# Eight feed-forward tiles narrowed among the experts, the second product two steps behind, five load buffers, remainders on VectorE

## The chip, the cores and the metric

The kernel runs on one NeuronCore of a Trainium2 chip. Its engines work side by side, each through its own instructions in order: TensorE (PE), VectorE (DVE), ScalarE (ACT), GpSimd (POOL) and SyncE (SP, which only issues transfers). The metric is the device time of one execution in microseconds (us), as a median of several runs. The profile is that of one execution.

## The reference

The program chains a linear attention with decay, a mixture of experts with one expert for each token, and a gated feed-forward layer. Only the last two are touched here:

```python
# x: 3072 tokens of width 512; 8 experts, w1 512x1024, w2 1024x512
for e in range(E):
    mask = e_idx == e
    h = np.maximum(x[mask] @ w1[e], 0.0)
    ye = h @ w2[e]
    out[mask] = gate_w[mask, None] * eom[mask, e, None] * ye
# then, with d_ff 1536
rms = np.sqrt(np.mean(x * x, axis=-1, keepdims=True) + 1e-06)
xn = x / rms * rms_g
g = xn @ w_gate
silu = g * (1.0 / (1.0 + np.exp(-g)))
val = xn @ w_val
return (silu * val @ w_out)
```

## The kernel before

All of it is one program whose order on each engine is the order in which the code is written. Products are made of three matmuls on 32-bit operands split into a rounded part (`h`) and a remainder (`l`): high times high, high times remainder, remainder times high. Four stages follow each other: attention with routing (0 to 157 us), the experts (157 to 463 us), the turn to the feed-forward layer, and the feed-forward layer itself on four pairs of blocks of 384 tokens.

**Experts.** The experts are taken in the order of their load, with `CAPS` = 448, 456, 432, 416, 408, 400, 384 and 368 columns for w = 0 to 7. Each has eight steps f. A step t = 8w + f is `up` (12 matmuls into PSUM bank f % 2, then ACT writes `hh` and DVE the remainder `hl`) and then `down` (12 matmuls into banks 4 to 7) of the step before. Behind f = 0 of the next expert `evac` copies banks 4 to 7 into `ys`. `settle` spreads the normalisation of the expert before over the steps: squares on ACT, sums and `halve` on DVE, `mean` (two matmuls with a tile of ones, then a square root on ACT) at f = 4, `inverse` (reciprocals on DVE) and `scale`. `turn` at f = 5 and 6 transposes the next expert's tokens.

**Expert weights.** Each of the 64 steps needs one weight tile of 128 x 1024. SP loads it into one of three buffers `raw`, ACT rounds it into slot `wt`, POOL writes the remainder beside it (`split_weights`). There are 12 slots; six lie outside the attention's memory.

**Feed-forward weights.** There are 36 tiles (j = 0 to 35) of 128 x 512 in 64-bit floating point, which arrive as pairs of integers and are narrowed on the chip: `narrow_steps` gives two ACT operations (L192, L193) and four DVE operations (L195, L201, L204, L207), and behind them come a rounding on ACT (L180) and a remainder on POOL (L181). Two tiles share a slot; tiles 3f, 3f + 1 and 3f + 2 make the weights of step f. Tiles 0 to 6 are narrowed during expert 7, tiles 7 to 13 in the turn, the rest in the first pair of blocks, three in each step f (`uconvs_to(17 + 3 * (f - 3), share)`, where a share says into how many parts the remaining work is still to be cut).

**Turn and feed-forward.** A step of a pair is `gate(b0, f)` (24 matmuls: 12 into bank 0, 12 into bank 1; ACT takes the silu of bank 0 in L825, DVE multiplies with bank 1 in L826, ACT rounds in L827, DVE makes the remainder in L828), `project` of the other block (9 matmuls), `gate(b1, f)` and `project(b0, f)`. So a gate's first half may start when ACT's L825 of the gate before has read bank 0, and its second half when DVE's L826 has read bank 1. In the turn the gates of steps 0 to 2 are interleaved with the last expert's normalisation (L369 is a reciprocal); its scaling is four multiplications on POOL (L964), once both reciprocals are there.

Of the kernel before, what the change touches and what calls it, by code (L numbers as in the profile page):

```python
# [25 lines left out]
KB = DM // 128  # L26
# [14 lines left out]
NPRE = 6  # L41
NSLOT = 12
NRAW = 3
NDIRECT = 4
# [60 lines left out]
def fused_kernel(  # L105
# [60 lines left out]
    def wslot(t):  # L166
        return wt[t % NSLOT if t < NWT + NSLOT else t - NWT]

# [17 lines left out]
    def narrow_steps(v, u, before):  # L186

        v = v.rearrange("p (c t) -> p c t", t=2)
        lo, hi, b = v[:, :, 0], v[:, :, 1], fl_b[0]

        def first():
            ACT.activation(out=u, in_=hi, func=AF.Abs, scale=2.0 ** -20)  # L192
            ACT.activation(out=u, in_=u, func=AF.Abs, bias=mid)  # L193
            before()
# [8 lines left out]
            ),  # L203
            lambda: DVE.scalar_tensor_tensor(  # L204
# [6 lines left out]

    state = {"load": 0, "work": 0, "end": NPRE}
    steps, after = [], []

    def loads_to(t):
        while state["load"] < min(t, state["end"]):
            n = state["load"]
            r = raw[n % NRAW]  # L220
            if n < NWT:
                load_expert_weights(r, window_expert(n // NF), n % NF)
            else:
                SP.dma_start(out=r.bitcast(I32), in_=wm2[n - NWT].bitcast(I32))
            state["load"] += 1

    def flush():
        for do in after:
            do()
        after.clear()  # L230

    def next_tile():
        n = state["work"]
        r = raw[n % NRAW]
        state["work"] += 1
        loads_to(n + NRAW - (n < NWT))
        if n < NWT:
            steps.append(lambda: split_weights(wslot(n), r))
        else:
            j = n - NWT  # L240
            u = fl_u[j % 2]
            narrow = narrow_steps(r.bitcast(I32), u, flush)
            last = lambda: after.append(lambda: split_weights(wslot(NWT + j // 2), u, j % 2))
            steps.extend([*narrow[:3], lambda: (narrow[3](), last())])

    def work_to(t, share=1):

        t = min(t, state["end"])
        left = len(steps) + sum(1 if n < NWT else 4 for n in range(state["work"], t))
        for _ in range(-(-left // share)):  # L250
            if not steps:
                next_tile()
            steps.pop(0)()

    def convs_to(t):
        work_to(min(t, NWT))

    def uconvs_to(n, share=1):
        work_to(NWT + n, share)
        if n >= NU and not steps:  # L260
            flush()


    class Experts:
# [41 lines left out]
        def up(self, w, f, n, wtile):  # L306
# [9 lines left out]
            hh, hl = self.hh[f % 2][:, 0:n], self.hl[f % 2][:, 0:n]  # L316
# [3 lines left out]
        def down(self, f, n, wtile):  # L320
            hh, hl = self.hh[f % 2][:, 0:n], self.hl[f % 2][:, 0:n]
# [120 lines left out]
    with ExitStack() as es:  # L442
# [335 lines left out]
        state["end"] = NWT + NU  # L778
# [33 lines left out]
    def gate(b, f, halves=None):  # L812
# [14 lines left out]
        ACT.activation(out=ah, in_=a, func=AF.Copy)  # L827
        DVE.tensor_tensor(out=al, in0=a, in1=f32(ah), op=ALU.subtract)  # L828
# [36 lines left out]
    hh = [m1.tile([128, CMAX], F32R, name=f"hh{i}") for i in range(2)]  # L865
    hl = [m1.tile([128, CMAX], F32R, name=f"hl{i}") for i in range(2)]
    ys = [m1.tile([128, KB, CMAX], F32, name=f"ys{i}") for i in range(2)]
    sq = [m1.tile([128, CMAX], F32, name=f"sq{i}") for i in range(KB)]
    ex = Experts(hh, hl, ys, sq, sq[1])
    pend = None  # L870

    def settle(w, f, bank):

        n = CAPS[w]
        if f == 0:
            ex.square(0, n)
            ex.square(1, n)
        elif f == 1:
# [267 lines left out]
```

## Time and profile before

| | |
|---|---|
| median of 3 runs (lowest, highest) | 1105.97 us (1104.77, 1106.41) |
| the profiled execution | 1100.29 us |
| its span, first to last instruction | 1098.6 us |
| PE busy | 1049.3 us (96%) |
| DVE busy | 505.8 us (46%) |
| ACT busy | 387.9 us (35%) |
| POOL busy | 336.7 us (31%) |
| mean granted clock of PE | 0.993 of full speed |

A busy PE is not yet a PE at its best pace: its matmuls are pipelined, so the pace is read from the distance of their starts. The idle time before an instruction and what ended it stand in brackets in a timeline. A share of busy time is a mean over stages with different limits, so each stage is read by itself.

### The profile page before, as it was taken

How to read it: one execution, taken by the hardware profiler on the slowest of the kernel's cores; microseconds unless marked ns; L12 is line 12 of the kernel's file. 1: busy time of each engine (PE TensorE's matmuls, PEld its weight loads, DVE VectorE, ACT ScalarE, POOL GpSimd, SP SyncE). 2: the span in 40 equal slices, each digit the busy share in tenths (PEclk: the TensorE clock that was granted, in tenths of full speed). 3: DMA queues.
4: the chain of work that ended last, by engine and by line, in shares of the span. 5: the costliest groups of instructions: out<-in, count | busy, mean ns of one | idle time of the engine just before them, and what ended most of it. 6: DMA issues, size and time to landing. Idle time of an engine off the chain costs nothing.

```text
span 1098.6 us, 16579 instructions
## 1 busy us (share of the span) xinstructions
PE 1049.3 (96%) x6537; PEld 973.3 (89%) x6538; DVE 505.8 (46%) x980; ACT 387.9 (35%) x742; POOL 336.7 (31%) x269
## 2 busy tenths in 40 slices
PE   6899989999999999898899999999999999999995
PEld 5787779989999999897888999999999999999995
DVE  3565652465665667988888631121321212212111
ACT  2443444453443454554555421111311112211111
POOL 2343457856646664624333220000110000200002
PEclk9999989999999999999999999999999999999998
DMA  7899746555645645533434120000200000100001
GB/s 267 231 261 251 191 119 199 151 162 166 201 151 165 205 153 164 148 103 102 135 120 127 64 88 8 1 1 1 87 29 1 1 1 30 58 1 1 1 1 61
DMA packets 47145, 115.43 MB, mean 105 GB/s; under 512 B 12893, under 2 KB 24413, under 8 KB 44242
## 3 DMA queue, kind: packets, MB, share of 16 engines
q1 hardware_dynamic: 39026, 96.01, 29.9%
q0 software_dynamic: 4864, 12.50, 3.2%
q10 hardware_dynamic: 3168, 5.77, 1.5%
q8 instruction: 53, 0.87, 0.3%
q14 instruction: 34, 0.28, 0.1%
HBM read 91.76 MB, written 23.11 MB: 105 GB/s over the span
## 4 chain that ended last, share of the span: by engine, by line
issue 40%; PE 37%; DVE 9%; ACT 4%; DMA 4%; POOL 3%; SPq 1%; POOLq 0%; DVEq 0%
PE ps L311 12%; PE ps L324 11%; DMA qkv<-att 3%; PE ps L818 3%; DVE fb L204 2%; PE ps L553 2%; POOL out_dram L851 2%; PE ps L525 2%; PE ps L519 1%; POOL w L181 1%; DVE fb L201 1%; PE ps L297 1%; PE ps L836 1%; PE ps L495 1%; ACT fu L192 1%
## 5 line engine op out<-in xcount | busy, mean ns | idle before, releaser
L818 PE MATMUL ps<-zh,w 128*128 128x384 f32 x960 | 257.0, 338 | 7.3 <-ACT a L825 7.3
L826 DVE TENSOR_TENSOR a<-a,ps 128x384 f32<-128x384 f32 x96 | 53.0, 552 | 322.5 <-PE ps L818 316.4
L818 PEld LDWEIGHTS ps<-zh,w 128*128 128x128 f32 x960 | 175.4, 189 | 12.9 <-ACT a L825 10.3
L181 POOL TENSOR_TENSOR w<-raw,w 128x1024 fp32r<-128x1024 f32 x64 | 155.7, 2447 | 91.5 <-ACT w L180 90.8
L818 PE MATMUL ps<-zl,w 128*128 128x384 f32 x480 | 161.8, 337 | 0.0
L818 PE MATMUL ps<-xh,w 128*128 128x384 f32 x576 | 154.8, 339 | 4.0 <-DVE a L826 2.6
L311 PE MATMUL ps<-xh,w 128*128 128x448 f32 (+7 forms) x512 | 149.7, 354 | 0.0
L836 PE MATMUL ps<-w,ah 128*128 128x512 f32 x564 | 145.3, 393 | 0.0
L851 POOL DMA_INDIRECT out_dram<-xw,perm x10 | 9.9, 992 | 420.6 <-ACT xw L849 417.6
L827 ACT ACTIVATE ah<-a 128x384 fp32r<-128x384 f32 x94 | 49.3, 525 | 202.9 <-DVE a L826 202.9
L836 PEld LDWEIGHTS ps<-w,ah 128*128 128x128 f32 x564 | 104.7, 188 | 16.3 <-ACT ys L346 0.4
L825 ACT ACTIVATE a<-ps 128x384 f32<-128x384 f32 x96 | 46.7, 487 | 201.4 <-PE ps L818 201.3
L818 PEld LDWEIGHTS ps<-xh,w 128*128 128x128 f32 x576 | 104.9, 188 | 7.3 <-DVE a L826 3.3
L324 PE MATMUL ps<-hh,w 128*128 128x448 f32 (+7 forms) x512 | 106.7, 350 | 0.0
L311 PEld LDWEIGHTS ps<-xh,w 128*128 128x128 f32 x512 | 95.3, 188 | 3.2
L818 PE MATMUL ps<-xl,w 128*128 128x384 f32 x288 | 97.0, 337 | 0.0
L324 PEld LDWEIGHTS ps<-hh,w 128*128 128x128 f32 x512 | 93.8, 188 | 2.9
L818 PEld LDWEIGHTS ps<-zl,w 128*128 128x128 f32 x480 | 90.7, 189 | 2.0
L311 PE MATMUL ps<-xl,w 128*128 128x448 f32 (+7 forms) x256 | 90.0, 351 | 0.0
L181 POOL TENSOR_TENSOR w<-fu,w 128x512 fp32r<-128x512 f32 x36 | 54.3, 1508 | 113.2 <-ACT w L180 113.2
L836 PE MATMUL ps<-w,al 128*128 128x512 f32 x282 | 80.0, 392 | 0.0
L828 DVE TENSOR_TENSOR al<-a,ah 128x384 fp32r<-128x384 f32 x94 | 52.5, 559 | 55.5 <-ACT ah L827 55.5
(151 smaller groups left out, 1441.6 us busy)
## 6 DMA issues: line engine op xcount, KB each, us to landing
raw<-wmoe SPq DMA_DIRECT2D x64, 512.0 KB, 3.8
qkv<-att SPq DMA_DIRECT2D x22, 1024.0 KB, 8.8
raw<-wm SPq DMA_DIRECT2D x36, 512.0 KB, 3.7
xw<-z SPq DMA_DIRECT2D x8, 768.0 KB, 5.3
xr<-row ACTq DMA_DIRECT2D x22, 256.0 KB, 9.5
z<-ys SPq DMA_DIRECT2D x2, 912.0 KB
z<-ys SPq DMA_DIRECT2D x2, 896.0 KB, 4.3
z<-ys SPq DMA_DIRECT2D x2, 864.0 KB
```

The lines of the kernel that those rows point to most:

```text
L181: POOL.tensor_tensor(out=dst[:, 1, c], in0=src, in1=f32(dst[:, 0, c]), op=ALU.subtract)
L204: lambda: DVE.scalar_tensor_tensor(out=b, in0=hi, scalar=-(1 << 30), in1=b, op0=ALU.bitwise_and, op1=ALU.bitwise_or),
L311: PE.matmul(p, lhsT=wtile[:, s, k * 128:(k + 1) * 128], rhs=x[w % len(xh)][:, k, 0:n], start=(i == 0), stop=(i == 3 * KB - 1),)
L324: PE.matmul(ps[:, 4 + k, 0:n], lhsT=wtile[:, s, 512 + k * 128:512 + (k + 1) * 128], rhs=h, start=(f == 0 and j == 0), stop=(f == NF - 1 an ...
L525: PE.matmul(o[64 * i:64 * i + 64, a], lhsT=vt[:, 2 * a + i], rhs=am[i][:, a], start=(c == 0 and a == 0), stop=True, skip_group_check=True,)
L818: PE.matmul(ps[:, part, 0:BT], lhsT=w2(f, part, s, k * 128, (k + 1) * 128), rhs=zz[:, k], start=(i == 0), stop=(i == 3 * KB - 1),)
L825: ACT.activation(out=a, in_=ps[:, 0, 0:BT], func=AF.Silu)
L826: DVE.tensor_tensor(out=a, in0=a, in1=ps[:, 1, 0:BT], op=ALU.mult)
L827: ACT.activation(out=ah, in_=a, func=AF.Copy)
L828: DVE.tensor_tensor(out=al, in0=a, in1=f32(ah), op=ALU.subtract)
L836: PE.matmul(ps[:, o_bank[b % 2][t]], lhsT=x[:, t * 128:(t + 1) * 128], rhs=w2(f, 2, s, 0, 512), start=(f == 0 and j == 0), stop=(f == NF2 ...
L851: ins = POOL.indirect_dma_start(out=out[:, :], out_offset=bass.IndirectOffsetOnAxis(ap=pm[:, t0 + t], axis=0), in_=o, in_offset=None, boun ...
```

## The change

- **Slots.** `NSLOT` is 11 (five outside the attention's memory, `NPRE`). From step 22 on the experts use seven of them in turn (`FEW`), and the other four take feed-forward tiles 0 to 7. One such tile is narrowed behind the expert tiles 27, 31, ..., 55, so in the first and the fifth step of experts 3 to 6.
- **Remainders.** The remainder of a feed-forward tile is made by DVE, between the second and the third narrowing step of the tile behind it; POOL has none any more. The two splits of feed-forward input (`z_split`) in expert 7 go from POOL to DVE as well.
- **Second product.** `down` runs two steps behind `up` (`BEHIND`), with three buffers for `hh` and `hl`; so `evac` stands behind f = 1.
- **Mean.** `mean` stands behind `up` at f = 5; the squares are all at f = 1, the reciprocals at f = 5 and 6, all four `scale` at f = 7.
- **Loads.** Two more buffers (`more`) while the experts run, so five; a load is issued as far ahead as buffers are free.
- **Pace.** Twelve tiles are done when expert 7 ends, five more in the turn, and the rest in the first pair at 2.5 tiles a step (`ready`); one narrowing step is put between L827 and L828 of each gate there.

The core of the diff:

```diff
-NPRE = 6
-NSLOT = 12
+NPRE = 5
+NSLOT = 11
 NRAW = 3
+NMORE = 2
+NFEW = 22
+FEW = 7
+BEHIND = 2
...
-        return wt[t % NSLOT if t < NWT + NSLOT else t - NWT]
+
+        if t < NFEW:
+            return wt[t % NSLOT]
+        if t < NWT:
+            return wt[t % FEW]
+        i = t - NWT
+        return wt[i + FEW if i < NSLOT - FEW else (t - NSLOT) % FEW if i < NSLOT else i]
...
+    def rest_of_weights(dst, src, c, eng):
+        eng.tensor_tensor(out=dst[:, 1, c], in0=src, in1=f32(dst[:, 0, c]), op=ALU.subtract)
...
+        ] + ([rest] if rest else []) + [
             lambda: DVE.scalar_tensor_tensor(
                 out=b, in0=hi, scalar=-(1 << 30), in1=b, op0=ALU.bitwise_and, op1=ALU.bitwise_or
             ),
...
+    def last_steps(j):
+        dst, c = half_slot(j)
+        u = fl_u[j % 2]
+        return lambda: round_weights(dst, u, c), lambda: rest_of_weights(dst, u, c, DVE)
...
+    jobs, nu = [], 0
+    for n in range(NWT):
+        jobs.append(("m", n))
+        if n >= NFEW + 4 and n % 4 == 3 and nu < 2 * (NSLOT - FEW):
+            jobs.append(("u", nu))
+            nu += 1
+    jobs += [("u", j) for j in range(nu, NU)]
...
+    def loads_to(t, spare=0):
+
         while state["load"] < min(t, state["end"]):
-            n = state["load"]
-            r = raw[n % NRAW]
-            if n < NWT:
+            i = state["load"]
+            room = [r for r in free if i < few_from or not any(r is x for x in more)]
+            if len(room) <= spare:
+                return
...
         ACT.activation(out=ah, in_=a, func=AF.Copy)
+        work(between)
         DVE.tensor_tensor(out=al, in0=a, in1=f32(ah), op=ALU.subtract)
...
             ex.up(w, f, n, wslot(t))
-            if pend is not None:
-                ex.down(pend[1], CAPS[pend[0]], wslot(pend[0] * NF + pend[1]))
-                if pend[1] == NF - 1:
-                    ex.evac(pend[0], CAPS[pend[0]])
-            pend = (w, f)
+            if w and f == 5:
+                ex.mean(w - 1, CAPS[w - 1], 2)
+            if t >= NFEW:
+                convs_to(t + FEW - BEHIND, 2)
+                if t + FEW - BEHIND > NWT:
+                    uconvs_to(nu + t + FEW - BEHIND - NWT, 2)
+            pend.append((w, f))
+            if len(pend) > BEHIND:
+                d = down_next()
+                if d[1] == NF - 1:
+                    ex.evac(d[0], CAPS[d[0]])
...
-                    z_split(1, POOL)
+                    z_split(1)
...
     gate(0, 1)
-    uconvs_to(9)
     ex.inverse(0, n // 2)
+    uconvs_to(14, 2)
     project(1, 0)
+    uconvs_to(14)
     gate(1, 1)
-    uconvs_to(11)
     ex.inverse(n // 2, n)
+    uconvs_to(15, 2)
     project(0, 1)
+    uconvs_to(15)
     gate(0, 2)
-    uconvs_to(12)
+    uconvs_to(16, 2)
     project(1, 1)
+    uconvs_to(16)
     gate(1, 2)
-    uconvs_to(13)
...
+    def ready(f):
+        return 17 + (f - 2) * 5 // 2
...
-            gate(b0, f)
+            early = int(p == 0 and state["work"] < len(jobs))
+            gate(b0, f, between=early)
             if p == 0:
-                uconvs_to(17 + 3 * (f - 3), 4)
+                uconvs_to(ready(f), 4)
```

Three places in the order of instructions follow. In them `fb` and `fu` are the buffers of narrowing, `hl` the remainder that `up` leaves, `ys` and `sq` the normalisation's tiles, `a`, `ah` and `al` what follows a gate.

DVE at the start of expert 4, from its first `hl` on, before:

```order
L318 SCALAR_TENSOR_TENSOR hl_1972<-ps,hh_1970 128x408
L335 COPY ys_1975<-ps 128x416 x2
L318 SCALAR_TENSOR_TENSOR hl_1973<-ps,hh_1971 128x408
L352 TENSOR_TENSOR sq_1976<-sq_1976,sq_1977 128x416
L318 SCALAR_TENSOR_TENSOR hl_1972<-ps,hh_1970 128x408
```

And DVE there now:

```order
L364 SCALAR_TENSOR_TENSOR hl_1974<-ps,hh_1971 128x408
L216 TENSOR_SCALAR fb<-more_1982 128x512
L222 SCALAR_TENSOR_TENSOR fb<-more_1982,fb 128x512
L192 TENSOR_TENSOR w_1949<-fu_72,w_1949 128x512
L226 SCALAR_TENSOR_TENSOR fb<-more_1982,fb 128x512
L229 SCALAR_TENSOR_TENSOR fu_71<-fu_71,fb 128x512
L364 SCALAR_TENSOR_TENSOR hl_1972<-ps,hh_1969 128x408
L381 COPY ys_1976<-ps 128x416 x2
```

One tile's narrowing, with the remainder of the tile before it (L192), stands between the first step's `hl` and the copies of `evac`, which moved behind the second step's.

DVE in the turn, from the gate of block 0, step 1, to that of block 0, step 2, before:

```order
L826 TENSOR_TENSOR a_1959<-a_1959,ps 128x384
L828 TENSOR_TENSOR al_1962<-a_1959,ah_1961 128x384
L195 TENSOR_SCALAR fb<-raw_68 128x512
L201 SCALAR_TENSOR_TENSOR fb<-raw_68,fb 128x512
L204 SCALAR_TENSOR_TENSOR fb<-raw_68,fb 128x512
L207 SCALAR_TENSOR_TENSOR fu_71<-fu_71,fb 128x512
L369 RECIPROCAL sq_1977<-sq_1977 128x184
L826 TENSOR_TENSOR a_1960<-a_1960,ps 128x384
L828 TENSOR_TENSOR al_1964<-a_1960,ah_1963 128x384
```

And the same place now, from that gate's L872 (L826 before) on, with two tiles ahead of the next gate's:

```order
L872 TENSOR_TENSOR a_1958<-a_1958,ps 128x384
L875 TENSOR_TENSOR al_1961<-a_1958,ah_1960 128x384
L415 RECIPROCAL sq_1978<-sq_1978 128x184
L216 TENSOR_SCALAR fb<-raw_68 128x512
L222 SCALAR_TENSOR_TENSOR fb<-raw_68,fb 128x512
L192 TENSOR_TENSOR w_89<-fu_72,w_89 128x512
L226 SCALAR_TENSOR_TENSOR fb<-raw_68,fb 128x512
L229 SCALAR_TENSOR_TENSOR fu_71<-fu_71,fb 128x512
L216 TENSOR_SCALAR fb<-more_1981 128x512
L222 SCALAR_TENSOR_TENSOR fb<-more_1981,fb 128x512
L192 TENSOR_TENSOR w_90<-fu_71,w_90 128x512
```

The reciprocal moved ahead of the narrowing, each tile got a fifth operation, and between the gates of blocks 0 and 1 stand two tiles instead of one.

POOL behind the last expert tile, before:

```order
L181 TENSOR_TENSOR w_90<-raw_68,w_90 128x1024
L807 TENSOR_TENSOR zl_1958<-xw,zh_1957 128x384 x4
L181 TENSOR_TENSOR w_91<-fu_71,w_91 128x512
L181 TENSOR_TENSOR w_91<-fu_72,w_91 128x512
L181 TENSOR_TENSOR w_92<-fu_71,w_92 128x512
```

And now:

```order
L192 TENSOR_TENSOR w_1947<-raw_70,w_1947 128x1024
L192 TENSOR_TENSOR w_1948<-raw_68,w_1948 128x1024
L192 TENSOR_TENSOR w_87<-raw_68,w_87 128x1024
L1022 TENSOR_TENSOR ys_1976<-ys_1976,sq_1978 128x368 x4
L897 MEMSET nop 1x1
```

The 36 remainders and the eight splits are gone from POOL; only the last expert's scaling (L964 before) is left between the experts and the output.

## Rows read from the trace of the kernel before

**Rows 1.** Stretches: busy time (x instructions) of each engine, PEclk, DMA share, GB/s.

```profile
457.34:527.38 70.04, 60.61 (x306) 54.25 (x306) 60.82 (x79) 39.35 (x68) 28.27 (x21) 0.98 0.36 102
527.38:609.46 82.08, 76.81 (x396) 70.21 (x396) 68.18 (x97) 44.81 (x78) 26.91 (x19) 1.00 0.45 135
628.35:653.31 24.96, 24.96 (x133) 23.50 (x132) 8.16 (x16) 8.20 (x17) 4.57 (x8) 1.00 0.34 106
275.00:440.00 165.00, 165.00 (x916) 162.11 (x917) 108.81 (x111) 77.44 (x127) 98.40 (x48) 1.00 0.56 174
```

**Rows 2.** Waits of PE, whole span: us in total, times, longest.

```profile
PE ps L818 <- ACT a L825: 8.7, 9, 2.0
PE ps L324 <- DVE hl L318: 3.2, 2, 2.3
PE ps L818 <- DVE a L826: 2.6, 2, 1.5
PE ps L365 <- DVE xl L360: 0.2, 1, 0.2
```

**Rows 3.** Chain of waits: start, us, what; an expert's down, a gate, a project.

```profile
436.96 2.00 PE ps L324 x12
615.99 4.21 PE ps L818 x24
620.21 2.04 PE ps L836 x9
```

**Rows 4.** PE's timeline: start, us, operation, [idle before it <- releaser].

```profile
466.37 0.94 PE L324 MATMUL ps<-hl,w 128*128 128x368 f32 x4 [2.30 <-DVE hl L318]
527.38 0.44 PE L818 MATMUL ps<-zh,w 128*128 128x384 f32 x1 [2.03 <-ACT a L825]
```

**Rows 5.** Stretches of 2 us behind PE's wait at 464, columns as in rows 1.

```profile
468.00:470.00 2.00, 2.00 (x8) 2.00 (x7) 1.86 (x3) 1.43 (x2) 0.16 (x1) 0.50 0.01 2
470.00:472.00 2.00, 1.97 (x9) 1.47 (x8) 2.00 (x4) 1.72 (x2) 1.02 (x1) 0.73 0.72 207
```

**Rows 6.** Groups by form, 440 to 680 us: busy, mean ns of one | idle before.

```profile
L195 DVE TENSOR_SCALAR fb<-raw 128x512 int32<-128x512 int32 x35 | 16.9, 482 | 0.5
L201 DVE SCALAR_TENSOR_TENSOR fb<-raw,fb 128x512 int32<-128x512 int32 x35 | 27.3, 779 | 1.2
L204 DVE SCALAR_TENSOR_TENSOR fb<-raw,fb 128x512 int32<-128x512 int32 x36 | 35.7, 993 | 1.0
L207 DVE SCALAR_TENSOR_TENSOR fu<-fu,fb 128x512 f32<-128x512 f32 x36 | 38.9, 1081 | 3.2
L828 DVE TENSOR_TENSOR al<-a,ah 128x384 fp32r<-128x384 f32 x31 | 17.3, 559 | 18.3 <-ACT ah L827 18.3
L826 DVE TENSOR_TENSOR a<-a,ps 128x384 f32<-128x384 f32 x31 | 17.0, 547 | 39.4 <-PE ps L818 33.4 <-ACT a L825 6.0
L369 DVE RECIPROCAL sq<-sq 128x184 f32<-128x184 f32 x2 | 2.6, 1289 | 0.0
L181 POOL TENSOR_TENSOR w<-fu,w 128x512 fp32r<-128x512 f32 x36 | 54.3, 1508 | 113.2 <-ACT w L180 113.2
```

**Rows 7.** Timelines of DVE and POOL in the turn to the feed-forward.

```profile
484.06 0.69 DVE L201 SCALAR_TENSOR_TENSOR fb<-raw,fb 128x512 int32<-128x512 int32 x1
485.07 1.57 POOL L181 TENSOR_TENSOR w<-fu,w 128x512 fp32r<-128x512 f32 x1 [12.69 <-ACT w L180]
485.59 1.60 DVE L207 SCALAR_TENSOR_TENSOR fu<-fu,fb 128x512 f32<-128x512 f32 x1
514.56 5.29 POOL L964 TENSOR_TENSOR ys<-ys,sq 128x368 f32<-128x368 f32 x4
516.32 1.33 DVE L201 SCALAR_TENSOR_TENSOR fb<-raw,fb 128x512 int32<-128x512 int32 x1
```

**Rows 8.** Timelines of DVE and POOL among the experts.

```profile
334.44 7.15 POOL L181 TENSOR_TENSOR w<-raw,w 128x1024 fp32r<-128x1024 f32 x3
336.84 5.21 DVE L360 TENSOR_TENSOR xl<-sq,xh 128x416 fp32r<-128x416 f32 x1
```

More of the change, by code (lines that the diff above doesn't have):

```diff
@@ new lines, in fused_kernel @@
+    jobs += [("u", j) for j in range(nu, NU)]
+    job_of = {job: i for i, job in enumerate(jobs)}
+    state = {"load": 0, "work": 0, "end": NPRE, "left": None}
+    steps = []
+    few_from = job_of["u", 16]
+    free, more, held = list(raw), [], {}
+    def loads_to(t, spare=0):
+        while state["load"] < min(t, state["end"]):
+            i = state["load"]
+            room = [r for r in free if i < few_from or not any(r is x for x in more)]
+            if len(room) <= spare:
+                return
+            kind, n = jobs[i]
+            r = held[i] = room[0]
+            free[:] = [x for x in free if x is not r]
+            if kind == "m":
@@ L238, in next_tile @@
+        loads_to(len(jobs), int(kind == "m"))
+        r = held.pop(i)
+        if kind == "m":
             steps.append(lambda: split_weights(wslot(n), r))
+            free.append(r)
         else:
[L240 to L244, printed above, removed]
+            steps.extend(narrow_steps(r.bitcast(I32), n, last_steps(n - 1) if n else (None, None)))
+            steps[-1:] = [lambda last=steps[-1]: (last(), free.append(r))]
+            if n == NU - 1:
+                steps.extend(last_steps(n))
@@ L246, in work_to, with work @@
+    def work(n):
+        for _ in range(n):
+            if not steps and state["work"] < len(jobs):
+                next_tile()
+            if steps:
+                steps.pop(0)()
     def work_to(t, share=1):
         t = min(t, state["end"])
[L249 to L256, printed above, removed]
+        left = len(steps) + sum(5 if kind == "u" else 1 for kind, _ in jobs[state["work"]:max(t, state["work"])])
+        if t == NWT + NU and left:
+            left += 2
+        work(-(-left // share))
@@ L258, in uconvs_to, with convs_to @@
+    def convs_to(t, share=1):
+        if t:
+            work_to(job_of["m", min(t, NWT) - 1] + 1, share)
     def uconvs_to(n, share=1):
-        work_to(NWT + n, share)
-        if n >= NU and not steps:
-            flush()
+        work_to(job_of["u", min(n, NU) - 1] + 1, share)
     class Experts:
@@ L777, in fused_kernel @@
         totals_b()
-        state["end"] = NWT + NU
+        state["end"] = len(jobs)
     wb = pool(ctx, "wb")
@@ L864, in fused_kernel, with down_next, settle @@
     xl.append(m1.tile([128, KB, CMAX], F32R, name="xl1"))
[L865 to L866 removed]
+    hh = [m1.tile([128, CMAX], F32R, name=f"hh{i}") for i in range(BEHIND + 1)]
+    hl = [m1.tile([128, CMAX], F32R, name=f"hl{i}") for i in range(BEHIND + 1)]
     ys = [m1.tile([128, KB, CMAX], F32, name=f"ys{i}") for i in range(2)]
     sq = [m1.tile([128, CMAX], F32, name=f"sq{i}") for i in range(KB)]
+    more.extend(m1.tile([128, 1024], F32, name=f"more{i}") for i in range(NMORE))
+    free.extend(more)
     ex = Experts(hh, hl, ys, sq, sq[1])
[L870 to L880 removed]
+    pend = []
+    def down_next():
+        w, f = pend.pop(0)
+        ex.down(w, f, CAPS[w], wslot(w * NF + f))
+        return w, f
+    def settle(w, f):
+        n = CAPS[w]
+        if f == 1:
+            for k in range(KB):
+                ex.square(k, n)
             ex.add(1, n, DVE)
@@ L981, in fused_kernel @@
             if p == 0:
-                uconvs_to(17 + 3 * (f - 3), 3)
-            gate(b1, f)
+                uconvs_to(ready(f), 3)
+            gate(b1, f, between=early)
             if p == 0:
-                uconvs_to(17 + 3 * (f - 3), 2)
+                uconvs_to(ready(f), 2)
             if f == 0:
@@ L990, in fused_kernel @@
             if p == 0:
-                uconvs_to(17 + 3 * (f - 3))
+                uconvs_to(ready(f))
                 if f == SETTLED:
                     ex.store(NE - 1, n, wpos(NE - 1), both(NE - 1))
+                    assert state["work"] > few_from
                     routed.close()
+                    free[:] = [r for r in free if not any(r is x for x in more)]
                     wc = pool(late, "wc")
```

78 lines of the change are left out of this document (36 added, 42 removed).

## The prediction

> **What bounds the kernel now.** I read the idle time of PE first, then what PE waits for, then the engine behind it. From 275 to 440 us, among the experts, PE is never idle: 165.00 of 165 us [rows 1]. Between 457.34 and 609.46 us, the end of expert 7, the turn and the first pair of blocks, it has 61 of 70 and 77 of 82 us, while DVE has 60.8 and 68.2 us of work there [rows 1]. PE's waits are all for what follows DVE: for the remainder `hl`, for the product L826, for the silu L825 [rows 2]. The silu is ACT's, but ACT takes its instructions in order, and ahead of it stands the rounding of a tile that DVE is still narrowing. So it is DVE that bounds this stretch, and PE everywhere else.
>
> What is lost there can be counted. Two undisturbed steps of a pair take 24.96 us, so 12.48 us each [rows 1]. From 527.38 to 609.46 us lie six steps in 82.08 us: 82.08 - 6 x 12.48 = 7.2 us. From 457.34 to 527.38 us lie three `down` and one `up` of 2.0 us each, eight gates and seven projects (three and a half steps of 12.48 and a gate of 4.21), and a `mean` of about 0.35 us: 8.0 + 43.7 + 4.2 + 0.35 = 56.25 us in 70.04, so 13.8 us [rows 1, 3]. Together 21.0 us. It is more than the waits show: each restart of PE costs about 0.3 us beside its wait (in the six steps, 82.08 - 76.81 = 5.3 us idle but 7.2 us lost), and behind the longest wait, 2.30 us [rows 4], the clock falls to the lower of its levels, 1.2 GHz, for most of 3 us: 0.50 and 0.73 of full speed in two stretches of 2 us, 2 x 0.50 + 2 x 0.27 = 1.5 us [rows 5].
>
> **The eight tiles among the experts.** A tile costs DVE 0.48 + 0.78 + 0.99 + 1.08 = 3.33 us now [rows 6]. A part of that is not work: L201 and L207 take 0.69 us with POOL at rest, and 1.60 us when POOL's remainder of 1.57 us has begun before it [rows 7]. Without POOL a tile is 0.48 + 3 x 0.69 = 2.55 us, and with the remainder on DVE 2.55 + 0.69 = 3.24 us. For the remainder, an operation that DVE does not have in this form yet, the bounds are 0.56 us (L828, 384 columns instead of 512) and POOL's 1.51 us for the same form [rows 6]; I take 0.69 because DVE's two-input operations of 512 columns take that.
>
> Eight tiles leave the bound stretch and take 8 x 3.24 = 26 us of DVE's time among the experts, where it has 165 - 108.8 = 56 us free [rows 1]. They meet POOL's expert remainders of 2.4 us, one in a step of an `up` and a `down`, about 4.4 us: a run of three of them held one DVE operation for 5.21 us [rows 8]. One such operation lost per tile makes 3.24 + 2.4 = 5.6 us, and 8 x 5.6 = 45 us still fit into 56. What hides a delay is the second product two steps behind: `hl` of step f is wanted only after a `down`, an `up`, another `down` and another `up` instead of after one `up`; each is 2.0 us at 368 columns [rows 3], so about 2.2 at 400. The one tight place is `evac`: the tile in an expert's first step stands ahead of the copies in the second, and the next `down` comes only one `up` (2.2 us) after the one that they empty. I put 0.5 us down for the four such places; it is at least 0 and at most 4 x (2.4 + 0.3) = 11 us.
>
> The Trainium skill, SBUF — State Buffer, "Who interferes with whom", says that DVE and GpSimd share one pair of ports as an exclusive lock, that whichever starts first holds it for its whole instruction, and that a DVE operation with two SBUF inputs needs it. By that a DVE operation waits for one POOL instruction at most; the wait of 5.21 us against 2.4 for one POOL instruction is longer [rows 8]. By the rule the experts cost 0, by the row up to the bound above.
>
> **The last expert and the turn.** Expert 7 narrows four tiles instead of seven, and POOL is free then, so the waits of its `down` (3.2 us, [rows 2]) and the slow clock behind them go; `hl` has one more step. The two splits now on DVE are 8 operations like L828, 8 x 0.56 = 4.5 us, against 3 x 3.33 = 10 us that leave.
>
> What is late next I look for gate by gate. From the end of gate (0, 1) to the moment when gate (1, 2) needs bank 1, PE has two and a half further gates and three projects: 2.5 x 4.2 + 3 x 2.05 = 16.7 us. Ahead of the L826 that frees the bank, DVE has two gates' ends of 0.55 + 0.56 + 0.5 (waiting for ACT between them) = 1.6 us, two reciprocals of 1.29, three tiles of 3.24, its own 0.55, and 0.6 until the first silu is there: 3.2 + 2.6 + 9.7 + 0.55 + 0.6 = 16.7 us [rows 3, 6]. That is level, and POOL's four multiplications of the last expert come on top: they become ready with the second reciprocal, and during their 5.29 us DVE gets one operation in for each, 1.33 instead of 0.69 us [rows 7]. 4 x 0.64 = 2.6 us, and with the restart 2.9 us of PE, stay. Behind that each gate has one tile (1.6 + 3.24 = 4.9 of 6.2 us), and DVE catches up. I leave another 0.7 us for waits too short for this sum.
>
> **The first pair.** 2.5 tiles and two gates' ends take DVE 2.5 x 3.24 + 2 x 1.1 = 10.3 us of 12.48; at the old 3.33 plus 0.69 it would be 12.3 us. So PE sets the pace even then, and the 7.2 us go. In a step of three tiles it is 3 x 3.24 + 2.2 = 11.9 us, still inside. ACT's work is the same; its rounding now waits for a DVE that is ahead.
>
> The Trainium skill, Perfetto Trace Analysis, "Optimizing Scalar/DVE Operations", would have work taken from a saturated DVE to GpSimd, the opposite of moving the remainders, and adds that the read port they share may spoil it. By its first half the remainders burden the engine that is the bound and the 7.2 us of the first pair stay, 1096.1; the 1.60 us beside POOL [rows 7] bear out the second.
>
> **Edits that cost nothing.** The mean a step later ends one wait of 0.2 us [rows 2]. Eight loads move ahead of 440 us, where the transfers use 0.56 of their time [rows 1]. On SP, the lists and the stores of normalised tokens queue behind loads; with five buffers these wait less for POOL, and tokens are wanted four steps after their list, so nothing waits. If a load came late, ACT's first operation on it would hold up `hh`; two steps of slack cover that. One slot fewer outside the attention's memory moves a conversion by a step, with tile 5 wanted five steps later.
>
> **Sum.** 21.0 + 0.2 - (2.9 + 0.7 + 0.5) = 17.1 us less than the profiled execution's 1100.3, so 1083.2 us. The median of the runs is 1106.0, 5.7 us above that execution; the stretch of the change is the same work in both, so I take the difference from the median: 1088.9 us.
>
> **The rivals.**
> - All of it goes: POOL's multiplications fall into a gap of DVE and `evac` is in time. 21.2 us: 1084.8. For it speaks that the turn's sum is level without POOL; against it that the second reciprocal releases POOL just as DVE begins a tile.
> - The turn stays bound by DVE: tiles stay at 3.33 + 0.69 = 4.0 us, so three of them are 2.3 us longer, and ACT's silu is late behind roundings in four gates by 1 us each with restarts. About 7 us stay besides: 1096. The waits on L825, 8.7 us in all [rows 2], speak for it; that POOL, which made tiles long, is idle there, against.
> - The copies of `evac` are late at all four places by one POOL instruction: 11 us, 1099.4. The mechanism is that of [rows 8], but one POOL operation in a step leaves DVE time between.
> - Slower: narrowing among the experts passes POOL more than once for each tile. DVE has 56 - 26 = 30 us left there, 3.8 us a tile; each us of waiting beyond that is 8 us of PE, since no slack of steps holds a lasting deficit. At 3.8 + 2.1 = 5.9 us of waiting, two and a half POOL operations, the gain of 17 us is eaten; with one such wait for each of four operations, 9.6 us, it costs 46 us and the time is 1135. [rows 8] speak for it (two POOL operations passed one of DVE's); that only one POOL operation of 2.4 us falls into 4.4 us speaks against.
> - The change doesn't do what it says: the tiles' time is only moved, and PE waits in the experts as long as it gains later. Then about 1106.
>
> **How the numbers follow.** My forecast has 0.50, all of it 0.17, the turn bound 0.17, late `evac` 0.06, slower 0.07, no effect 0.03. The range is from 1084 (all of it) to 1097 (the turn bound), which holds 0.84; the bounds of the remainder's price (28 x 0.8 us, of which the first pair can hide most) lie inside it. Faster by over 0.2%, which is about what a measurement of this kernel can tell, 0.90; within that 0.03; slower 0.07.
>
> **What would show it.** Right: steps of 12.5 us in the first pair; DVE's L222, L226, L229 at 0.69 us there; no wait of PE in expert 7 and no clock below 1; one wait of 2 to 3 us before the second half of gate (1, 2), with L1022 on POOL beside tile 14. Wrong: PE waiting among experts 3 to 6 at the `down` behind `evac`, narrowing operations of 2 us and more there, or remainders far from 0.69 us.

## The result, and the profile after

The changed kernel takes 1086.66 us (median of 4 runs, 1086.22 to 1088.41) against 1105.81 us of the kernel before beside it: ratio 0.9834, interval 0.9812 to 0.9856, so 19.2 us less. The forecast was 17.1 us less, 1088.9 us. The profiled execution took 1086.34 us, its span is 1084.5 us.

PE's pace shows where the time went. I read the starts of PE's blocks from its timeline and cut the span at four of them: the first `up`, the first gate of the turn, its seventh gate (the first of the first pair), and the gate fourteen further on (seven steps of the pair).

| profiled kernel | attention | experts | turn | seven pair steps | rest | from the first `up` on |
|---|---|---|---|---|---|---|
| before | 157.5 | 309.6 | 42.6 | 99.8 | 489.1 | 941.1 |
| after | 162.2 | 305.8 | 39.6 | 87.7 | 489.2 | 922.4 |
| after, second profile | 161.8 | 305.8 | 39.6 | 87.7 | 489.1 | 922.3 |

So 18.7 us are gone behind the first `up`: 3.8 among the experts (expert 7's waits of [rows 2]), 3.0 in the turn, 12.0 in the pair. The attention is left out of the comparisons below, since it differs between executions of the same code: it ends between 159.7 and 168.8 us in eleven profiles of the changed kernel and its versions, on several chips (between 160.2 and 163.8 us in four of them on one chip).

PE's waits after, from 175 to 640 us (us in total, times, longest), answer to [rows 2]; of all of them one is left, and it is a new one:

```profile
PE ps L864 <- DVE a L872: 1.5, 1, 1.5
```

The stretches after (columns as in [rows 1]): among the experts, the turn, the seven steps of the pair.

```profile
280.00:445.00 165.00, 165.00 (x916) 162.33 (x916) 131.87 (x147) 90.70 (x150) 103.63 (x49) 1.00 0.66 203
467.95:507.54 39.59, 38.06 (x204) 35.89 (x204) 31.48 (x49) 20.58 (x35) 5.15 (x5) 1.00 0.20 60
507.54:595.27 87.73, 87.73 (x463) 82.46 (x462) 67.52 (x119) 47.32 (x83) 0.00 (x0) 1.00 0.41 126
```

PE has no gap in the first and the third. The third is 87.73 / 7 = 12.53 us a step, against 99.77 / 7 = 14.25 before. DVE's work among the experts has risen from 108.81 to 131.87 us without a wait of PE, and the granted clock stays at 1.00, where [rows 5] had 0.50.

DVE's narrowing after, by form: the first four rows are the pair's (507.54 to 595.27 us), the last two the experts' (280 to 445 us). Columns: busy us, mean ns of one | idle before. Here L216, L222, L226, L229 are the four narrowing operations and L192 the remainder.

```profile
L229 DVE SCALAR_TENSOR_TENSOR fu<-fu,fb 128x512 f32<-128x512 f32 x18 | 12.4, 691 | 0.5
L192 DVE TENSOR_TENSOR w<-fu,w 128x512 fp32r<-128x512 f32 x18 | 12.4, 690 | 5.6 <-ACT w L189 5.6
L222 DVE SCALAR_TENSOR_TENSOR fb<-raw,fb 128x512 int32<-128x512 int32 x18 | 12.4, 688 | 0.2
L226 DVE SCALAR_TENSOR_TENSOR fb<-raw,fb 128x512 int32<-128x512 int32 x17 | 11.6, 685 | 0.0
...
L229 DVE SCALAR_TENSOR_TENSOR fu<-fu,fb 128x512 f32<-128x512 f32 x8 | 20.1, 2510 | 0.4
L226 DVE SCALAR_TENSOR_TENSOR fb<-more,fb 128x512 int32<-128x512 int32 x8 | 9.9, 1241 | 0.0
```

The remainder (L192) costs the 0.69 us that I had taken. Among the experts the last two operations wait for POOL, 2.51 and 1.24 us instead of 0.69. With the 0.69, 0.69 and 0.41 of the others a tile is 5.5 us; I had forecast 5.6.

The one wait is where it was forecast, in the second half of gate (1, 2). DVE, POOL and PE there, in their timelines:

```profile
495.66 1.30 DVE L415 RECIPROCAL sq<-sq 128x184 f32<-128x184 f32 x1
497.27 1.35 DVE L222 SCALAR_TENSOR_TENSOR fb<-more,fb 128x512 int32<-128x512 int32 x1
498.54 1.46 DVE L192 TENSOR_TENSOR w<-fu,w 128x512 fp32r<-128x512 f32 x1
499.92 1.46 DVE L226 SCALAR_TENSOR_TENSOR fb<-more,fb 128x512 int32<-128x512 int32 x1
501.42 1.34 DVE L229 SCALAR_TENSOR_TENSOR fu<-fu,fb 128x512 f32<-128x512 f32 x1
502.68 0.54 DVE L872 TENSOR_TENSOR a<-a,ps 128x384 f32<-128x384 f32 x1
...
497.09 5.12 POOL L1022 TENSOR_TENSOR ys<-ys,sq 128x368 f32<-128x368 f32 x4 [45.48 <-ACT w L189]
...
503.28 0.45 PE L864 MATMUL ps<-xh,w 128*128 128x384 f32 x1 [1.53 <-DVE a L872]
```

The second reciprocal releases POOL's four multiplications; beside them each of DVE's four operations takes 1.34 to 1.46 us, and L872, which frees bank 1, comes 1.5 us late. The gate takes 5.99 us instead of 4.2, so 1.8 us; I had put 2.9 down.

### The profile page after: what moved, and what is told of

Read it like the earlier page. It is cut to its first block, busy times and chain, and to the rows that moved or that the text cites. A ratio compares the mean times of both kernels' runs of the same rounds, so it can differ in the third digit from the quotient of the medians.

```text
span 1084.5 us, 16504 instructions
## 1 busy us (share of the span) xinstructions
PE 1044.3 (96%) x6537; PEld 973.8 (90%) x6538; DVE 498.0 (46%) x1024; ACT 386.5 (36%) x742; POOL 274.2 (25%) x225
## 5 line engine op out<-in xcount | busy, mean ns | idle before, releaser
L872 DVE TENSOR_TENSOR a<-a,ps 128x384 f32<-128x384 f32 x96 | 53.2, 554 | 332.9 <-PE ps L864 332.2
L357 PE MATMUL ps<-xh,w 128*128 128x448 f32 (+7 forms) x512 | 149.8, 354 | 0.3 <-DVE hl L364 0.3
L192 POOL TENSOR_TENSOR w<-raw,w 128x1024 fp32r<-128x1024 f32 x46 | 115.0, 2504 | 79.9 <-ACT w L189 73.6
L357 PEld LDWEIGHTS ps<-xh,w 128*128 128x128 f32 x512 | 95.2, 188 | 3.8 <-DVE hl L364 0.6
L357 PE MATMUL ps<-xl,w 128*128 128x448 f32 (+7 forms) x256 | 89.7, 351 | 0.0
L363 ACT ACTIVATE hh<-ps 128x448 fp32r<-128x448 f32 (+7 forms) x64 | 33.0, 515 | 111.1 <-PE ps L357 108.6
```

The source lines that it names most:

```text
L192: eng.tensor_tensor(out=dst[:, 1, c], in0=src, in1=f32(dst[:, 0, c]), op=ALU.subtract)
L357: PE.matmul(p, lhsT=wtile[:, s, k * 128:(k + 1) * 128], rhs=x[w % len(xh)][:, k, 0:n], start=(i == 0), stop=(i == 3 * KB - 1),)
L363: ACT.activation(out=hh, in_=p, func=AF.Relu)
L872: DVE.tensor_tensor(out=a, in0=a, in1=ps[:, 1, 0:BT], op=ALU.mult)
```

## The experiments

Each table row is one profiled execution, cut as above; the medians are those of its own runs, beside 1105.5 to 1105.8 us of the kernel before (for the last three it is one run beside 1106.2 to 1109.7).

| kernel | time | ratio (interval) | experts | turn | seven pair steps | from the first `up` on |
|---|---|---|---|---|---|---|
| remainders alone | 1094.86 | 0.9891 (0.9857 to 0.9924) | 309.2 | 40.1 | 92.8 | 931.2 |
| all but the remainders | 1086.48 | 0.9831 (0.9801 to 0.9862) | 305.8 | 38.8 | 89.5 | 922.9 |
| all but the tiles, first attempt | 1098.03 | 0.9923 (0.9900 to 0.9947) | 314.4 | 40.2 | 89.6 | 934.0 |
| all but the tiles, second | 1095.79 | 0.9915 (0.9885 to 0.9946) | 311.3 | 43.2 | 88.5 | 932.6 |
| one step behind | 1088.68 | 0.9848 (0.9803 to 0.9893) | 307.4 | 40.7 | 87.7 | 925.1 |
| small edits undone | 1093.58 | 0.9914 (0.9880 to 0.9948) | 313.6 | 39.6 | 87.7 | 930.9 |
| multiplications later | 1083.38 | 0.9811 (0.9783 to 0.9839) | 305.8 | 37.8 | 87.7 | 920.6 |
| changed kernel again | 1085.82 | 0.9831 (0.9806 to 0.9856) | 305.8 | 39.6 | 87.7 | 922.3 |
| narrowing, three more | 1105.20 | - | 325.8 | 39.6 | 87.7 | 942.4 |
| narrowing, six more | 1133.45 | - | 353.0 | 39.6 | 87.7 | 969.6 |
| three more, other steps | 1104.72 | - | 317.7 | 39.6 | 87.7 | 934.2 |

**The remainders alone**, in the kernel before:

```diff
-        POOL.tensor_tensor(out=dst[:, 1, c], in0=src, in1=f32(dst[:, 0, c]), op=ALU.subtract)
+        eng = POOL if half is None else DVE
+        rest = lambda: eng.tensor_tensor(out=dst[:, 1, c], in0=src, in1=f32(dst[:, 0, c]), op=ALU.subtract)
...
+            while rests:
+                rests.pop(0)()
```

> The kernel before, with one edit alone: the remainder of each narrowed tile is an operation of DVE, behind the tile's second operation, instead of one of POOL; the eight tiles stay where they were. Theory A (POOL beside DVE is what stretches the tiles): with POOL at rest a tile is 2.55 + 0.69 = 3.24 us, three of them and two gates' ends 11.9 us, so the steps of the first pair go from 13.68 to 12.5 us and 7 to 9 us are gained: 1097 to 1099 us. Rival B (DVE's load is what counts): a tile costs DVE 3.24 instead of 3.33 us, which is nearly the same; the pair's steps stay above 13.3 us and less than 2 us are gained: 1104 us or more.

Measured: 10.9 us gained by the medians and 9.9 from the first `up` on (941.1 - 931.2), more than theory A's 7 to 9. DVE took on an operation a tile and the bound stretch became shorter. Two stretches of the same length, 527.21 to 603.77 us, before and with this edit:

```profile
527.21:603.77 76.56, 72.03 (x373) 66.14 (x374) 63.40 (x90) 41.10 (x73) 25.11 (x17) 1.00 0.43 127
```

```profile
527.21:603.77 76.56, 76.54 (x396) 70.24 (x396) 66.51 (x115) 44.86 (x78) 0.00 (x0) 1.00 0.48 144
```

These are six steps with the edit, 12.76 us each. PE's 4.5 us of idle time are gone, POOL is at rest, and DVE does 115 operations instead of 90 in 3 us more. Rival B falls. What stays are the last expert (a wait of 3.1 us for `hl`) and the backlog of the turn, which the pair's first step carries.

**All but the remainders**, the changed kernel with one word changed:

```diff
-        return lambda: round_weights(dst, u, c), lambda: rest_of_weights(dst, u, c, DVE)
+        return lambda: round_weights(dst, u, c), lambda: rest_of_weights(dst, u, c, POOL)
```

> The changed kernel with the remainders back on POOL. Theory A (the eight tiles moved and the slack of two steps carry the gain): 2.5 tiles of 3.33 us and 2.2 us of gates' ends are 10.5 us of a pair step of 12.5, so the pair stays at PE's pace; the turn has tiles of 3.33 instead of 3.24 us; 1086 to 1089 us. Rival B (POOL beside DVE is what cost the time): the turn, level with the remainders on DVE, is late again, and the first pair's steps leave 12.5 us: 1091 us or more.

Measured: the same time as the changed kernel. Beside POOL the narrowing is slow as before (the pair, 517 to 593.8 us, by form):

```profile
L229 DVE SCALAR_TENSOR_TENSOR fu<-fu,fb 128x512 f32<-128x512 f32 x15 | 19.5, 1299 | 1.0
L226 DVE SCALAR_TENSOR_TENSOR fb<-raw,fb 128x512 int32<-128x512 int32 x15 | 12.6, 837 | 0.4
...
L192 POOL TENSOR_TENSOR w<-fu,w 128x512 fp32r<-128x512 f32 x16 | 22.2, 1385 | 55.3 <-DVE fb L226 30.2 <-ACT w L189 22.9 <-DMA raw<-wm 2.1
```

L229 takes 1.30 instead of 0.69 us, but with 2.5 tiles a step DVE has room for it. One place in the pair costs 1.8 us (89.5 instead of 87.7), and the turn, where DVE has one operation less a tile, gives back 0.8. Theory A holds: with the eight tiles moved and the other edits in place, it does not matter whose the remainders are.

**All but the tiles.** No tile among experts 3 to 6, the pace of the kernel before. In the first attempt the last three expert tiles were all converted in expert 7's second step, and PE waited 3.5 and 2.0 us for them; one of them also overwrites an earlier tile before the last product with it, so one product of that run takes wrong weights. The second attempt spreads them:

```diff
-        if n >= NFEW + 4 and n % 4 == 3 and nu < 2 * (NSLOT - FEW):
+        if n >= NWT - 3:
...
-            if t + FEW - BEHIND > NWT:
-                uconvs_to(nu + t + FEW - BEHIND - NWT)
+            if t > NWT - NF:
+                uconvs_to(t - NWT + NF)
```

> The changed kernel with no tile narrowed among experts 3 to 6; the number of tiles that are done by each gate is that of the kernel before. Remainders on DVE, two steps of slack, the buffers and the splits on DVE stay. Theory A (the eight tiles are the gain of the last expert and the turn): 8 x 3.24 = 26 us of DVE come back there, most of its 13.8 us come back with them, and the first pair stays near 12.5 us a step: 1096 to 1100 us. Rival B (shorter tiles and two steps of slack are enough): 1087 to 1089 us.

> As the run before without tiles among experts 3 to 6, but with the last three expert tiles converted in their own steps and not all at the first step of expert 7, which had cost PE two waits of 5.4 us there for reasons of its own. Theory A (the eight tiles are the gain of the last expert and the turn, 8 x 3.24 = 26 us of DVE): 1096 to 1100 us still. Rival B (with shorter tiles and two steps of slack the stretch holds all but a few of the us; the eight tiles are worth what the earlier run lost without its two waits): 1091 to 1094 us. Rival C (the eight tiles are worth nothing beside the other edits): 1087 to 1089 us.

Measured: 1095.79 us, just below theory A's range and 1.8 us above rival B's. PE's waits in the second attempt, 175 to 640 us:

```profile
PE ps L357 <- DVE hl L364: 3.7, 1, 3.7
PE ps L864 <- ACT a L871: 3.2, 2, 2.8
PE ps L864 <- DVE hl L364: 0.2, 1, 0.2
```

Without the eight tiles all the rest of the change brings 8.5 us from the first `up` on (941.1 - 932.6), somewhat less than the remainders bring alone. So the tiles are worth 10.3 us beside the other edits (932.6 - 922.3). That is a price beside these edits and not of the tiles alone: the wait of 3.7 us stands behind a stretch in which DVE has both a tile and one of the splits that the change gave to it (3.75 us from 448.41 us on), and behind the two longest waits the granted clock is at 0.50, the lower of its two levels (460 to 462 and 511 to 513 us). The two ways are not a sum: the remainders alone 9.9, the tiles with everything else 18.2, both 18.7 us, all from the first `up` on.

**One step behind**, the conversions' look-ahead kept:

```diff
-BEHIND = 2
+BEHIND = 1
+LOOK = 5
...
-    down_next()
     gate(0, 0)
     down_next()
```

> The changed kernel with the second product one step behind again; the conversions keep their look-ahead of five tiles, and the tiles among the experts stay. Theory A (two steps are the cover that the prediction named): a tile of 5.5 us on DVE stands in two portions ahead of hl, which is then wanted after one up of 2.2 us instead of 6.6; each of the eight tiles costs PE 1 to 3 us, and expert 7's waits of about 3 us come back: 1097 to 1110 us. Rival B (the portions of half a tile fit beside one up): no more than 3 us, 1086 to 1090 us.

Measured: 1088.68 us, rival B; theory A falls. The second step is worth 2.8 us (925.1 against 922.3): three short waits in the experts and one in the turn.

```profile
PE ps L371 <- DVE hl L365: 1.0, 3, 0.6
PE ps L865 <- DVE hl L365: 0.6, 1, 0.6
```

**Small edits undone**: three load buffers, the last expert's splits on POOL, the mean behind the `up` of step 4.

```diff
-NMORE = 2
+NMORE = 0
...
-            if w and f == 5:
+            if w and f == 4:
...
-                    z_split(0)
+                    z_split(0, POOL)
...
-                    z_split(1)
+                    z_split(1, POOL)
```

> The changed kernel with three small edits undone: three load buffers instead of five, the last expert's two splits on POOL, the mean at step 4 of the next expert instead of 5. Theory A (they cost and bring nothing, as the prediction has it): within 1 us of the changed kernel. Rival B (the loads need the buffers): a tile among the experts waits for its load, ACT's queue stands, and PE waits at hh by 1 us or more for each of several tiles: 1089 us or more. Rival C (the splits on POOL hold up DVE in expert 7): 1 to 4 us there, 1087.5 to 1090 us.

Measured: 1093.58 us, 7.8 more than the changed kernel beside it, and 7.8 more in the experts; so theory A falls. PE's waits name the mean; below them one of the four places in the timelines of DVE, POOL and PE:

```profile
PE ps L411 <- DVE xl L406: 6.2, 4, 2.0
...
341.40 3.64 DVE L406 TENSOR_TENSOR xl<-sq,xh 128x416 fp32r<-128x416 f32 x1 [1.11 <-ACT xh L405]
...
339.84 4.74 POOL L192 TENSOR_TENSOR w<-raw,w 128x1024 fp32r<-128x1024 f32 x2
...
343.26 0.35 PE L357 MATMUL ps<-xh,w 128*128 128x408 f32 x1
343.44 0.35 PE L411 MATMUL ps<-xh,ones 128*128 128x416 f32 x1
345.09 0.46 PE L411 MATMUL ps<-xl,ones 128*128 128x416 f32 x1 [1.30 <-DVE xl L406]
```

From the mean's start to the next block it is 2.74, 1.95, 2.51 and 1.72 us instead of 0.39: 7.4 of the 7.8 us that the experts lose. The halves of the mean (L406) are DVE's last step at f = 3; here they are held beside POOL's remainders and come too late. But this run does not put the mean back where it stood. It has the mean behind the `up` (L357) of step 4 and ahead of a `down`; in the kernel before it stood behind that `down` (L324), as PE's timeline shows at the same expert:

```profile
341.55 0.91 PE L324 MATMUL ps<-hl,w 128*128 128x408 f32 x4
342.30 0.35 PE L365 MATMUL ps<-xh,ones 128*128 128x416 f32 x1
```

A `down` is 2.1 to 2.3 us at these columns, and the mean lost 2.35, 1.56, 2.12 and 1.33 us; so in its old place it would have been late by about 0.1 us at one place and in time at the others. That is an estimate from these distances, not a run. The 7.4 us are the price of a place that neither kernel has.

Rival B has a part in it. What ACT waits for a load, 280 to 445 us, and the longer of its two waits in its timeline:

```profile
ACT w L189 <- DMA raw<-wmoe: 4.4, 2, 2.5
300.33 1.06 ACT L189 ACTIVATE w<-raw 128x1024 fp32r<-128x1024 f32 x1 [2.53 <-DMA raw<-wmoe]
```

With three buffers ACT stands 2.5 and 1.9 us for a tile's load ahead of the rounding of `xh` (L405), at two of the four places, and there L406 starts 2.5 and 1.9 us behind the start of the `up` of step 4 instead of with it. In the changed kernel ACT waits for no load in that window. So the buffers bring something beside a mean that stands this early; what they bring beside the mean in its old or new place no run shows. No wait names a split.

**Multiplications later**: the second reciprocal and POOL's four operations in the first step of the pair.

```diff
-    ex.inverse(n // 2, n)
     uconvs_to(15, 2)
...
-    for k in range(KB):
-        POOL.tensor_tensor(out=ex.ys[:, k, 0:n], in0=ex.ys[:, k, 0:n], in1=ex.sqt[:, 0:n], op=ALU.mult)
     project(0, 2)
...
+                if f == 3:
+                    ex.inverse(n // 2, n)
+                    for k in range(KB):
+                        POOL.tensor_tensor(out=ex.ys[:, k, 0:n], in0=ex.ys[:, k, 0:n], in1=ex.sqt[:, 0:n], op=ALU.mult)
```

> The changed kernel with the last expert's second reciprocal, and so POOL's four multiplications, moved from the turn into the first step of the first pair. Theory A (POOL's multiplications beside tile 14 and the reciprocal ahead of it are what holds bank 1 at gate (1, 2)): the wait of 1.53 us there goes, the gate takes 4.2 instead of 5.99 us, and the multiplications hide in the pair, where DVE has some 2 us of each step free: 1.8 us less than the changed kernel, 1084.8 us. Rival B (the wait only moves to the next gate): within 0.5 us of the changed kernel.

> The changed kernel as it is, beside the other runs on one chip: 1086.3 to 1087 us. What differs from its first profile before the first up is the attention's variation from execution to execution; the time from the first up to the end should agree within 0.5 us.

Measured: 1083.38 against 1085.82 us beside it. The runs spread more widely (1080.51 to 1088.91 and 1083.47 to 1090.06) than these differ, as the attention's end does between profiles; the stages tell the two apart: the turn is 37.81 instead of 39.60 us, the pair the same. Turn and pair in this kernel:

```profile
466.03:503.84 37.81, 37.81 (x205) 35.95 (x204) 28.87 (x51) 21.77 (x38) 0.00 (x0) 1.00 0.24 73
503.84:591.57 87.73, 87.73 (x463) 82.46 (x462) 69.86 (x117) 46.23 (x81) 5.19 (x5) 1.00 0.40 122
```

PE waits for nothing any more between 440 and 640 us. Theory A holds: 1.8 us expected, 39.60 - 37.81 = 1.79 us measured. The changed kernel itself came out as in its first profile, 922.3 and 922.4 us from the first `up` on. In the pair POOL's 5.19 us still stretch DVE's operations, and nobody waits. By the stages it is the fastest version here (920.6 us from the first `up` on).

**More narrowing among the experts**: the second operation of each of the eight tiles is repeated three or six times, to the same result.

```diff
+            for _ in range(3 * again):
+                DVE.scalar_tensor_tensor(
+                    out=b, in0=lo, scalar=29, in1=b, op0=ALU.logical_shift_right, op1=ALU.bitwise_or
+                )
```

> The changed kernel with three more operations of DVE for each of the eight tiles among the experts: the second operation of the narrowing is done four times, to the same result. At 0.69 to 1.24 us each that is 2.1 to 3.7 us a tile, 17 to 30 us of DVE, of which 33 us are free between 280 and 445 us. Theory A (the slack of two steps and DVE's free time hide it; only a lasting deficit costs PE): no more than 2 us over the changed kernel's time from the first up to the end, 922.4 us. Rival B (the copies of evac, which stand with 0.44 us to spare at one expert, are late at each of four experts by 2 to 3.5 us): 8 to 14 us more, with PE waiting at the first down behind evac.

> As the run before, with six more operations a tile: 4.1 to 7.4 us, 33 to 60 us of DVE in all. Theory A (only a deficit beyond the 33 free us costs PE, then us for us): 0 to 27 us over the changed kernel. Rival B (each expert's evac is late by the whole delay): 4 x 4.1 to 4 x 7.4, 16 to 30 us, all of it at the first down behind evac. Where the waits of PE stand (at hl by then, or at evac alone) tells the two apart.

Measured: 20.0 and 47.2 us more in the experts. PE's waits with three more, DVE's repeated operation (by form, 280 to 460 us), and the stretches behind three of the four waits (columns as in [rows 1]):

```profile
PE ps L375 <- DVE ys L386: 12.3, 4, 3.8
...
L226 DVE SCALAR_TENSOR_TENSOR fb<-more,fb 128x512 int32<-128x512 int32 x24 | 42.0, 1748 | 0.8
...
296.00:302.00 6.00, 6.00 (x24) 5.62 (x23) 4.57 (x5) 2.50 (x5) 4.14 (x3) 0.72 1.01 372
382.00:386.00 4.00, 3.97 (x13) 3.75 (x13) 3.17 (x5) 2.74 (x5) 1.74 (x2) 0.57 0.91 319
422.00:432.00 10.00, 7.77 (x29) 7.77 (x30) 7.15 (x10) 3.39 (x7) 4.58 (x4) 0.66 0.92 270
```

The six groups of a tile add up to 9.5 us instead of 5.5 (12.0 with six more). All four waits stand at the `down` behind `evac`, for DVE's copies `ys`: rival B's place, at a higher price. Waits of 12.3 us cost 20.0, because the clock falls: behind PE's waits of 2.3, 3.2 and 3.8 us, though not behind that of 2.9, the granted clock is at 0.50, the lower of its two levels (1.2 GHz), for a while, and the `up` behind two of them takes 3.2 instead of 2.2 us. By the three rows that is 6 x 0.28 + 4 x 0.43 + 10 x 0.34 = 6.8 us, a third of the cost, which no theory had; the 0.9 us that are left are the four restarts. Theory A falls: DVE's 33 free us are not free to use. With six more the copies' waits are 20.2 us, the transposes of the next expert's tokens wait for DVE too, 9.6 us, and the mean granted clock of the experts' 353 us is 0.94, where the changed kernel has 1.00.

**Three more, in other steps**: is it that place?

```diff
-        if n >= NFEW + 4 and n % 4 == 3 and nu < 2 * (NSLOT - FEW):
+        if n >= NFEW + 4 and n % 4 == 1 and nu < 2 * (NSLOT - FEW):
```

> The run with three more operations a tile, and the eight tiles handed out two steps later, so that none of them stands in an expert's first step, ahead of the copies of evac. DVE's work among the experts is the same. Theory A (the place ahead of evac is what costs, and elsewhere two steps of slack hide 9 us of DVE a tile): the four waits for ys go, and of the 20 us over the changed kernel's 922.4 us from the first up to the end no more than 4 are left. Rival B (DVE's time among the experts is used up, the four waits are only where the deficit shows): 15 us or more stay, now before hl or the mean.

Measured: between the two, 11.9 us in the experts. The waits for `ys` are gone, and others have come:

```profile
PE ps L362 <- DVE hl L369: 6.7, 4, 2.2
...
385.77 5.47 DVE L226 SCALAR_TENSOR_TENSOR fb<-raw,fb 128x512 int32<-128x512 int32 x1
385.91 2.42 POOL L192 TENSOR_TENSOR w<-raw,w 128x1024 fp32r<-128x1024 f32 x1
388.27 2.41 POOL L192 TENSOR_TENSOR w<-more,w 128x1024 fp32r<-128x1024 f32 x1
394.82 0.49 PE L362 MATMUL ps<-xh,w 128*128 128x400 f32 x1 [1.82 <-DVE hl L369]
```

It is an `up` (L362) that waits for `hl`, not a `down`: `up` of step t + 2 writes the PSUM bank f % 2 from which `hl` of step t is still to be made. A tile costs DVE 8.1 us here, since POOL meets it less, so the extra work is 2.6 x 8 = 21 us where it was 32 us; PE lost 11.9 and 20.0 us, about 0.6 us for each in both; of these 6.7 and 12.3 are waits and 3.4 and 6.8 the clock (here its mean is 0.72 from 394 to 400 and from 434 to 440 us). So the place decides where PE waits, and not clearly how much: outside `evac` too there is room for little more than a tile of 5.5 us.

## Why the prediction was right, point by point

- **The stretch and its size.** Right: 21.0 us were said to be lost before; 18.7 went with the change and 20.5 with the later multiplications (941.1 - 920.6). By the prediction's own cut, at the gate of 527.38 us (520.11 after), 11.9 us went ahead of it and 6.9 behind it; the forecast was 13.8 - 3.6 = 10.2 and 7.2.
- **The eight tiles among the experts.** Right in price (5.5 us a tile, 5.6 forecast) and in effect (no wait). At `evac` I put 0.5 us down; it cost nothing, by a small margin. In a tight place, DVE, POOL and PE in their timelines, the copies end at 371.54 and the `down` that overwrites their banks starts at 371.98; at the next expert it is 408.12 and 408.35:

```profile
367.29 2.79 DVE L229 SCALAR_TENSOR_TENSOR fu<-fu,fb 128x512 f32<-128x512 f32 x1
370.48 1.06 DVE L381 COPY ys<-ps 128x408 f32<-128x408 f32 x2
...
366.76 5.59 POOL L192 TENSOR_TENSOR w<-raw,w 128x1024 fp32r<-128x1024 f32 x2 [3.83 <-ACT w L189]
...
371.98 1.25 PE L370 MATMUL ps<-hh,w 128*128 128x400 f32 x6
```

- **What hides a delay.** Wrong in count. I had `hl` wanted after four blocks instead of one. The runs show the bank of `up` as the earlier tie: it is three blocks (`down`, `up`, `down`) with two steps. With one step it is a `down` (which I had left out), an `up` and the first eight of the twelve matmuls of the next `down`, for only the last four read `hl`. A third of a block more is little, and the second step is worth 2.8 us by the run with one step behind, not the whole cover that I gave it.
- **The last expert and the turn.** Right in place and cause; the four multiplications cost 1.8 us where I had 2.9: the sum of 2.6 was right for DVE (four operations 5.6 instead of 2.8 us), but DVE had about 1.3 us in hand where I had it level. The 0.7 us for small waits did not come.
- **The first pair.** Right: 12.53 us a step at 0.69 us an operation, and with the remainders on POOL PE waits at one place only, as the sum of 10.5 us ahead of that run had said. The remainders alone bring 9.9 us from the first `up` on, and nothing once the tiles are gone. So the Trainium skill, Perfetto Trace Analysis, "Optimizing Scalar/DVE Operations", by which giving some work of a saturated DVE to GpSimd may make sense, is not borne out by the run with the remainders alone: work taken from GpSimd to the busy DVE shortened the stretch. The page's own caveat on their shared port is. In the changed kernel the move either way is worth nothing.
- **Edits that cost nothing.** Right for the changed kernel as it stands: the mean's wait of 0.2 us is gone, and PE waits for no load and no split. That the edits are worth nothing is not shown. The run that undoes them is 7.4 us dearer at the mean, but with the mean one `down` ahead of its old place (the change had moved it one `up` behind that place), so it says nothing of the 0.2 us. Nor does the mean's input come later than before: at experts 3 to 6 the halves end 3.0 to 3.9 us after the start of the `up` of step 4, and before they ended 3.7 to 4.2 us after it. For the buffers the term of nothing is open: with three, a load came late twice and held up `xh`, where I had looked at `hh` alone.
- **The slower rival.** Its price was near and its mechanism wrong. It let a tile wait 3.8 us for free and cost 8 us for each further one; by that the tile of 9.5 us with three more operations costs (9.5 - 3.24 - 3.8) x 8 = 20 us, and 20.0 were measured. That is chance: of the 20.0 us 6.8 are the clock, which the rule does not have, and PE waited at four places instead of in a lasting deficit. With six more the same rule gives 40 us where 47.2 were measured. With a tile of 8.1 us it gives 8.5, and 11.9 were measured.
- **Sum.** 17.1 us forecast, 18.7 by the stages, 19.2 by the medians. The difference is 1.1 us of POOL, 0.7 of small waits and 0.5 of `evac` that were not lost, less 0.7 that I can't place. Taking the shift of the profile to the median as the attention's is borne out: the first `up` of the profile before stands at 157.5 us, earlier than in any other profile here.

## What to carry to other kernels

Two cures of one bound stretch, less work in it and faster operations in it, are not a sum: before adding both, ask what the second still has to cure. Free time of an engine is worth only what the nearest buffer or bank lets pass; count the blocks up to the next write of that bank, not those up to the next reader. A run that undoes an edit must put the moved work back exactly where it stood: one block further ahead the mean cost 7.4 us, which say nothing of its old place. And a wait of PE can cost more than its length, by what the clock does behind it.

## What the hardware showed

- A DVE operation that starts 0.14 us ahead of POOL's (385.77 against 385.91) was passed by two POOL operations and ended 0.56 us behind the second: 5.47 us instead of 0.69. In another place a DVE operation started at 367.29 beside a POOL operation of 2.8 us that had started at 366.76; that one passed, and DVE's took 2.79 us. The Trainium skill, SBUF — State Buffer, "Who interferes with whom", has whoever issues first hold the port pair for the whole instruction; by the starts in the profile the first place does not agree with that, the second does.
- Beside four POOL operations in a row DVE gets one operation in for each, 1.34 to 1.46 us, as in [rows 7].
- Behind PE's waits of 2.3, 3.2 and 3.8 us among the experts the granted clock was at 0.50 for a while (mean 0.72, 0.57 and 0.66 over 6, 4 and 10 us), and not behind a wait of 2.9 us; three waits of together 9.3 us cost 6.8 us more by it.
- The same attention code ended between 159.7 and 168.8 us in eleven profiles, more than most of the effects here; only stages behind it can be compared to a microsecond.
